# Weight conversion in two pieces through PSUM, small values in spare PSUM columns, and a new order of the work

## The chip, the cores and the metric

The kernel runs on one core of a Trainium2 chip. The time is the device time of one execution in microseconds (us); of the kernel before there are three runs, with a median of 528.46 us. Engines are called PE (TensorE), DVE (VectorE), ACT (ScalarE), POOL (GpSimd) and SP (the engine that issues the loads). Of the engines only PE, DVE and ACT work on PSUM here; POOL works on SBUF.

## The reference

Three stages follow each other on 1536 tokens (2 batches of 768) of width 320 (8 heads of 40).

```python
# stage 1: mLSTM, per batch and head, over 768 steps (written as a recurrence)
m_new = max(f + m, i);  f_s = exp(f + m - m_new);  i_s = exp(i - m_new)
C = f_s * C + i_s * outer(v, k);  n = f_s * n + i_s * k
y = sigmoid(o) * (C @ q) / max(|n . q|, 1)
# stage 2: x (1536 x 320), w_in (320 x 2048), w_out (2048 x 320)
h = x @ w_in
g = (a0 + a1*h + a2*h^2 + a3*h^3) / (1 + |b0|*|h| + |b1|*h^2 + 1e-6)
x = g @ w_out
# stage 3: w_gate, w_val (320 x 1536), w_out2 (1536 x 320)
xn = x / sqrt(mean(x*x) + 1e-6) * rms_g
out = (silu(xn @ w_gate) * (xn @ w_val)) @ w_out2
```

The weights lie in memory as 64-bit floating-point numbers (two 32-bit words for each value). The kernel makes 32-bit values of them, and of each of those a high and a low part for TensorE.

## The kernel before

**Weights.** There are 34 pieces of weight: 8 of `w_in` (key `"i"`), 8 of `w_out` (`"o"`), 12 of gate and value (`"2"`) and 6 of `w_out2` (`"3"`). Each has 640 values in each of 128 partitions and goes through `weight` (line 287): a load of 640 KB into a `raw` buffer; `c0` (line 301) and `c1` (line 307) on DVE, which shift and mask the upper word into a `cv` buffer of 640 elements; and the third step `c2`. For the 16 weights `"i"` and `"o"` it is an addition on POOL (line 325) of rounding bits that ACT prepared (`carry`, line 319); for the 18 others it is a third DVE instruction (line 312) that brings in bits of the lower word. Then ACT writes the high part (line 329) and POOL the low part (line 333). `raw` and `cv` lie in SBUF. So 34 `c0`, 34 `c1` and 18 `c2` run on DVE, each over 640 elements with every operand in SBUF.

**Attention.** 12 chunks of 128 tokens (`chunk`, line 420). A chunk has matmuls into banks named `pf`, `ps`, `pi`, `py`, `pu` and `pt`; two scans on DVE (line 435), two products (line 457); and the denominators `den_` (line 515): an absolute value on ACT, then a maximum and a reciprocal on DVE (lines 516 to 518), all in the SBUF tile `den` with 8 values in a partition. POOL uses the result in `rs` (line 522). Bank `py` goes back once `yd` has added it into the SBUF tile `yb`.

**Pairs.** Stage 2 is 48 pairs (`pair`, line 599) of 256 tokens by 256 inner columns. Each has 16 matmuls into one bank `h`, a chain on ACT, POOL and DVE, and 12 matmuls into two accumulators `acc`. Five DVE instructions of a pair (lines 645, 647, 653, 655, 657, called p2, p3, w, y2 and g) have 512 elements; p3 reads what p2 wrote, and g reads what y2 wrote. Pairs of the first two token blocks alternate, so four banks are accumulators at first, and two later on.

**Norm.** After the last pair of each of 6 blocks, `rms` (line 667): squares and a first inverse root on ACT; `newton` with five DVE instructions of two values each, in the SBUF tile `few` (lines 682 to 686); scaling on ACT (line 690), weighing on POOL, a store.

**Units.** Stage 3 is `unit` (line 754), with 512-column banks `g0` and `g1`, and sums into `acc2`.

**What sets the order.** All work is a list of 1825 tasks, and `ORDER` (line 22) is a fixed list of their numbers. Each engine runs its own tasks in that order, one after the other; SP issues loads in that order too. A task may `take` a buffer from a ring and another may `give` it back. The eight PSUM banks are one ring `"b"`; a bank is taken from the front and returned at the back, so that its next taker waits until the last one is done with it.

Of the kernel before, what the change touches and what calls it, by code (L numbers as in the profile page):

```python
# [11 lines left out]
I32 = mybir.dt.int32  # L12
# [101 lines left out]
def kernel(  # L114
# [75 lines left out]
    def T(*name):  # L190
        return held[name][1]
# [95 lines left out]
    def weight(key, src, dst, how, after=(), room=()):  # L287
# [12 lines left out]
        def c0():  # L300
            DVE.tensor_scalar(  # L301
                out=cv(), in0=words()[..., 1], scalar1=3, scalar2=0x3FFFFFFF,
                op0=ALU.logical_shift_left, op1=ALU.bitwise_and,
            )
# [702 lines left out]
```

## Time and profile before

| | us |
|---|---|
| runs: median (lowest to highest) | 528.46 (527.77 to 529.08) |
| profiled execution: its own time | 526.69 |
| its span, first to last instruction | 524.8 |
| PE busy | 464.4 |
| DVE busy | 370.1 |
| ACT busy | 305.4 |
| POOL busy | 327.9 |

Busy time is the part of the span in which an engine had at least one instruction running. Two instructions of one engine may overlap by a little in the records, so that a sum of durations can exceed the busy time. The times in the rows below count from the start of the span. A "slot" in this document is the time from the start of one DVE instruction to the start of the next.

### The profile page before, as it was taken

The page shows a single profiled execution, that of the slowest core. Times are in us where ns is not written, and L with a number is a line of the kernel's source. Part 1 is how long each engine was busy: PE and PEld are TensorE (multiplying, and loading weights), DVE is VectorE, ACT ScalarE, POOL GpSimd, SP SyncE. Part 2 cuts the span into 40 slices and gives each one's busy share as a digit, 9 for nine tenths or more (in the row PEclk, how much of TensorE's full clock was granted, in tenths as well). Part 3 has the DMA queues.
Part 4 walks back from the last instruction along what each step waited for, and adds up shares of the span by engine and source line. Part 5 has one row for each costly group of instructions (what it writes and reads, how often), then busy time and mean ns, then how long its engine had stood idle before and what let it go on. Part 6 is the DMA issues. An engine that isn't in the chain of part 4 may idle for free.

```text
span 524.8 us, 9403 instructions
## 1 busy us (share of the span) xinstructions
PE 464.4 (88%) x3616; PEld 429.3 (82%) x3616; DVE 370.1 (71%) x564; ACT 305.4 (58%) x565; POOL 327.9 (62%) x324
## 2 busy tenths in 40 slices
PE   0688976785999899998788989999999999999997
PEld 0577966675887889898687979989898988989997
DVE  7998898989999999999999999777611121111112
ACT  4243787677997787788988999583312222231112
POOL 3698887997988777678787695666750130311220
PEclk9999978898999999999999999999999999999999
DMA  8755624311012123204021115433101000000002
GB/s 255 243 145 160 205 94 136 99 59 51 26 44 65 35 56 108 70 7 139 37 82 51 51 30 179 156 96 129 56 31 50 0 14 26 1 1 9 5 1 76
DMA packets 18365, 40.40 MB, mean 77 GB/s; under 512 B 3952, under 2 KB 11904, under 8 KB 18320
## 3 DMA queue, kind: packets, MB, share of 16 engines
q1 hardware_dynamic: 18320, 39.80, 24.4%
q8 instruction: 28, 0.46, 0.4%
q14 instruction: 17, 0.14, 0.1%
HBM read 35.86 MB, written 3.93 MB: 76 GB/s over the span
## 4 chain that ended last, share of the span: by engine, by line
PE 40%; DVE 31%; ACT 17%; issue 6%; DMA 2%; POOL 2%; SPq 0%; DVEq 0%; ACTq 0%; POOLq 0%
PE bank L773 22%; PE bank L783 4%; PE bank L782 4%; PE bank L781 4%; DVE bank L655 3%; DVE z L653 3%; DVE vv L647 3%; DVE vv L645 3%; DVE cv L301 3%; DVE w_buf L435 3%; PE bank L617 3%; DVE cv L307 3%; ACT bank L650 3%; DVE vv L657 2%; ACT z L641 2%
## 5 line engine op out<-in xcount | busy, mean ns | idle before, releaser
L617 PE MATMUL bank<-xt,win 128*128 128x256 f32 x768 | 109.7, 300 | 20.1 <-DVE vv L657 10.2
L617 PEld LDWEIGHTS bank<-xt,win 128*128 128x128 f32 x768 | 102.8, 205 | 24.4 <-DVE vv L657 11.3
L849 DVE TENSOR_TENSOR vv<-bank,vv 128x512 f32<-128x512 f32 x35 | 23.7, 688 | 95.1 <-PE bank L773 80.7
L644 POOL TENSOR_TENSOR z<-z,u 128x512 f32<-128x512 f32 x48 | 64.1, 1335 | 21.7 <-ACT z L641 20.0
L661 POOL TENSOR_TENSOR gl<-vv,gh 128x512 fp32r<-128x512 f32 x48 | 64.7, 1352 | 10.9 <-ACT gh L660 6.7
L627 PE MATMUL bank<-wou,gh 128*128 128x320 f32 x192 | 60.2, 325 | 5.3 <-ACT gh L660 2.6
L629 PE MATMUL bank<-wou,gh 128*128 128x320 f32 x192 | 58.9, 318 | 0.8 <-POOL wou L333 0.8
L846 ACT ACTIVATE vv<-bank 128x512 f32<-128x512 f32 x35 | 20.8, 597 | 59.9 <-PE bank L773 51.0
L855 POOL TENSOR_TENSOR wou<-vv,wou 128x512 fp32r<-128x512 f32 x18 | 24.4, 1362 | 41.4 <-ACT wou L852 39.8
L627 PEld LDWEIGHTS bank<-wou,gh 128*128 128x128 f32 x192 | 37.6, 196 | 6.8 <-ACT gh L660 3.3
L650 ACT ACTIVATE bank<-z,few 128x512 f32<-128x512 f32 x48 | 32.8, 686 | 15.5 <-DVE vv L647 14.0
L641 ACT ACTIVATE z<-u,few 128x512 f32<-128x512 f32 x48 | 39.1, 814 | 2.1 <-DVE vv L657 1.0
L307 DVE SCALAR_TENSOR_TENSOR cv<-raw,cv 128x640 int32<-128x640 int32 x34 | 39.9, 1184 | 0.3
L629 PEld LDWEIGHTS bank<-wou,gh 128*128 128x128 f32 x192 | 37.5, 195 | 1.4 <-POOL wou L333 1.4
L627 PE MATMUL bank<-wou,gl 128*128 128x320 f32 x192 | 37.9, 320 | 0.8 <-POOL gl L661 0.6
L643 ACT ACTIVATE vv<-bank,few 128x512 f32<-128x512 f32 x48 | 32.3, 679 | 7.9 <-PE bank L617 3.2
L645 DVE SCALAR_TENSOR_TENSOR vv<-vv,few,bank 128x512 f32<-128x512 f32 x48 | 35.5, 740 | 1.5 <-ACT vv L643 0.7
L647 DVE SCALAR_TENSOR_TENSOR vv<-vv,few,bank 128x512 f32<-128x512 f32 x48 | 35.6, 743 | 0.8
L655 DVE SCALAR_TENSOR_TENSOR bank<-vv,few,bank 128x512 f32<-128x512 f32 x48 | 35.8, 747 | 0.1
L660 ACT ACTIVATE gh<-vv 128x512 fp32r<-128x512 f32 x48 | 29.7, 623 | 9.3 <-DVE vv L657 9.2
L333 POOL TENSOR_TENSOR win<-cv,win 64x128 fp32r<-64x128 f32 (+2 forms) x37 | 29.7, 803 | 7.9 <-ACT win L329 6.1
L653 DVE SCALAR_TENSOR_TENSOR z<-z,bank 128x512 f32<-128x512 f32 x48 | 32.4, 678 | 2.1 <-ACT bank L652 1.6
(156 smaller groups left out, 1163.7 us busy)
## 6 DMA issues: line engine op xcount, KB each, us to landing
raw<-in_w_out_dram SPq DMA_DIRECT2D x14, 640.0 KB, 5.0
raw<-in_w_gv_dram SPq DMA_DIRECT2D x12, 640.0 KB, 4.6
raw<-in_w_in_dram SPq DMA_DIRECT2D x8, 640.0 KB, 5.1
lqk<-in_qk_tr_dram SPq DMA_DIRECT2D x24, 192.0 KB, 4.0
lv<-in_v_dram SPq DMA_DIRECT2D x12, 160.0 KB, 4.2
los<-in_o_gate_dram SPq DMA_DIRECT2D x12, 160.0 KB, 3.3
lk<-in_k_dram SPq DMA_DIRECT2D x12, 160.0 KB, 3.2
z_dram<-rnd SPq DMA_DIRECT2D x6, 320.0 KB, 3.1
```

Of the source, the lines that this page charges most:

```text
L307: DVE.scalar_tensor_tensor(out=cv(), in0=words()[..., 1], scalar=-0x40000000, in1=cv(), op0=ALU.bitwise_and, op1=ALU.bitwise_or)
L617: PE.matmul(out=hb()[:, e], lhsT=l, rhs=r, start=(x == 0), stop=(x == len(mm) - 1))
L627: PE.matmul(out=o, lhsT=l, rhs=woh[:, f], start=first, stop=last)
L629: PE.matmul(out=o, lhsT=l, rhs=wol[:, f], start=False, stop=False)
L641: go("z", lambda: ACT.activation(out=z(), in_=u(), func=ACTF.Identity, scale=babs[:, 1:2], bias=babs[:, 0:1]), [("hu", i)], ["z"])
L644: go("zu", lambda: POOL.tensor_tensor(out=z(), in0=z(), in1=u(), op=ALU.mult), [("z", i)], [], ["u"])
L645: go("p2", lambda: DVE.scalar_tensor_tensor(out=vv(), in0=vv(), scalar=nacoef[:, 2:3], in1=hb(), op0=ALU.add, op1=ALU.mult), [("hu", i), ( ...
L647: go("p3", lambda: DVE.scalar_tensor_tensor(out=vv(), in0=vv(), scalar=nacoef[:, 1:2], in1=hb(), op0=ALU.add, op1=ALU.mult), [("p2", i)])
L650: go("ars", lambda: ACT.activation(out=hb(), in_=z(), func=ACTF.Abs_reciprocal_sqrt, bias=cq), [("zu", i), ("p3", i)])
L655: go("y2", lambda: DVE.scalar_tensor_tensor(out=hb(), in0=vv(), scalar=nacoef[:, 0:1], in1=hb(), op0=ALU.add, op1=ALU.mult), [("w", i)])
L661: go("gl", lambda: POOL.tensor_tensor(out=gl(), in0=vv(), in1=r32(gh()), op=ALU.subtract), [("gh", i)], ["gl"], ["vv"])
L773: PE.matmul(out=bank(i, e), lhsT=l, rhs=r, start=y == 0, stop=y == len(mm) - 1)
```

## The change

Four edits.

First, `c0`, `c1` and `c2` on DVE are each made twice over 320 elements. What lies between them (`mid`) is no longer in the SBUF buffer `cv` but in columns 0 to 319 of a PSUM bank that the piece takes from ring `"b"` at `c0` and gives back at its last DVE step. The last step writes `cv`. One operand, the word that was loaded, still comes from SBUF. The ACT step `carry` no longer comes after `c0`.

Second, the denominators' absolute value and maximum lie in columns 336 to 343 of bank `py`, which is now given back after the reciprocal; the three instructions become three tasks.

Third, in `newton` the mean's scaling and the first square go to ACT, and the three instructions left on DVE work on two columns of the accumulator bank.

Fourth, `ORDER` is a new list, of 1953 tasks.

```diff
+        def word(x, t):
+            return piece(T(*rk)[:, 0:1280].rearrange("p (m t) -> p m t", t=2)[..., t], x)
+        def mid(x):
+            return T("cb", key, x)[:, 0:320].bitcast(I32)
-        def c0():
+        def c0(x):
             DVE.tensor_scalar(
-                out=cv(), in0=words()[..., 1], scalar1=3, scalar2=0x3FFFFFFF,
+                out=mid(x), in0=word(x, 1), scalar1=3, scalar2=0x3FFFFFFF,
                 op0=ALU.logical_shift_left, op1=ALU.bitwise_and,
             )
-        def c1():
+        def c1(x):
             DVE.scalar_tensor_tensor(
-                out=cv(), in0=words()[..., 1], scalar=-0x40000000, in1=cv(), op0=ALU.bitwise_and, op1=ALU.bitwise_or
+                out=piece(T(*ck), x) if how > 0.5 else mid(x), in0=word(x, 1), scalar=-0x40000000, in1=mid(x),
+                op0=ALU.bitwise_and, op1=ALU.bitwise_or,
             )
-        def c2():
+        def c2(x):
             DVE.scalar_tensor_tensor(
-                out=cv(), in0=words()[..., 0], scalar=29, in1=cv(), op0=ALU.logical_shift_right, op1=ALU.bitwise_or
+                out=piece(T(*ck), x), in0=word(x, 0), scalar=29, in1=mid(x),
+                op0=ALU.logical_shift_right, op1=ALU.bitwise_or,
             )
...
+            task(("c0",) + key + (x,), lambda x=x: c0(x), [("ld",) + key] + old, take=[("b", ("cb", key, x))])
...
-            task(("cr",) + key, carry, [("c0",) + key], take=[("rnd", nk)])
+            task(("cr",) + key, carry, [("ld",) + key], take=[("rnd", nk)])
...
-        def den_():
-            ACT.activation(out=den, in_=T("yb", j)[:, :, D:D1], func=ACTF.Abs)
-            DVE.tensor_scalar(out=den, in0=den, scalar1=1.0, scalar2=None, op0=ALU.max)
-            DVE.reciprocal(out=den, in_=den)
+        def den_(x):
+            t = T("py", j)[:, 336:344, None]
+            if x == 0:
+                ACT.activation(out=t, in_=T("yb", j)[:, :, D:D1], func=ACTF.Abs)
+            elif x == 1:
+                DVE.tensor_scalar(out=t, in0=t, scalar1=1.0, scalar2=None, op0=ALU.max)
+            else:
+                DVE.reciprocal(out=den, in_=t)
...
+        def few_():
+            return T("acc", n, 0)[:, 336:338]
+            ACT.activation(out=ms, in_=ss, func=ACTF.Identity, scale=1.0 / DM, bias=eps6)
+            ACT.activation(out=few_(), in_=y, func=ACTF.Square)
         def newton():
-            DVE.tensor_scalar(out=ms, in0=ss, scalar1=1.0 / DM, scalar2=1e-6, op0=ALU.mult, op1=ALU.add)
-            DVE.tensor_tensor(out=t2, in0=y, in1=y, op=ALU.mult)
-            DVE.tensor_tensor(out=t2, in0=t2, in1=ms, op=ALU.mult)
-            DVE.tensor_scalar(out=t2, in0=t2, scalar1=-0.5, scalar2=1.5, op0=ALU.mult, op1=ALU.add)
-            DVE.tensor_tensor(out=t2, in0=t2, in1=y, op=ALU.mult)
+            t = few_()
+            DVE.tensor_tensor(out=t, in0=t, in1=ms, op=ALU.mult)
+            DVE.tensor_scalar(out=t, in0=t, scalar1=-0.5, scalar2=1.5, op0=ALU.mult, op1=ALU.add)
+            DVE.tensor_tensor(out=t2, in0=t, in1=y, op=ALU.mult)
```

## Rows read from the trace of the kernel before

**Rows 1.** The page: busy us (share of the span) of each engine, instructions

```profile
PE 464.4 (88%) x3616; PEld 429.3 (82%) x3616; DVE 370.1 (71%) x564; ACT 305.4 (58%) x565; POOL 327.9 (62%) x324
```

**Rows 2.** Busy time by stretch: length; PE, PEld, DVE, ACT, POOL; clock, DMA share, GB/s

```profile
50.00:150.00 100.00, 80.92 (x688) 75.49 (x685) 92.20 (x131) 76.31 (x135) 87.12 (x85) 0.90 0.28 90
150.00:250.00 100.00, 93.68 (x972) 86.89 (x971) 97.81 (x165) 80.39 (x151) 77.43 (x85) 1.00 0.24 72
250.00:316.00 66.00, 55.07 (x387) 51.93 (x385) 63.67 (x99) 57.88 (x113) 50.47 (x45) 0.97 0.16 48
350.00:525.00 175.00, 171.40 (x1004) 156.31 (x1002) 45.23 (x61) 44.91 (x83) 54.72 (x39) 1.00 0.10 32
```

**Rows 3.** Three DVE lines: count, min/median/max ns, first and last start

```profile
L301 DVE TENSOR_SCALAR cv<-raw x34: 473/789/1653, 8.5 to 375.8; 128x640 int32<-128x640 int32 x34
L307 DVE SCALAR_TENSOR_TENSOR cv<-raw,cv x34: 810/873/2143, 9.9 to 376.8; 128x640 int32<-128x640 int32 x34
L653 DVE SCALAR_TENSOR_TENSOR z<-z,bank x48: 635/680/690, 64.7 to 331.4; 128x512 f32<-128x512 f32 x48
```

**Rows 4.** Timeline of DVE and of POOL around 170 us: start, length

```profile
170.28 1.13 DVE L684 TENSOR_TENSOR few<-few 128x2 f32<-128x2 f32 x1
...
170.13 1.27 POOL L644 TENSOR_TENSOR z<-z,u 128x512 f32<-128x512 f32 x1
```

**Rows 5.** Instructions on tile cv by stretch: length; busy DVE, ACT, POOL

```profile
0.00:50.00 50.00, 10.21 (x12) 4.48 (x9) 17.46 (x14) 1.00 0.70 206
50.00:150.00 100.00, 23.35 (x21) 9.66 (x22) 36.42 (x33) 0.90 0.28 90
150.00:250.00 100.00, 7.16 (x6) 2.97 (x7) 6.15 (x6) 1.00 0.24 72
250.00:316.00 66.00, 16.42 (x18) 5.66 (x15) 13.54 (x18) 0.97 0.16 48
```

**Rows 6.** Groups by line and shape: busy us, mean ns | idle before

```profile
L301 DVE TENSOR_SCALAR cv<-raw 128x640 int32<-128x640 int32 x34 | 30.2, 902 | 0.2
L795 DVE COPY ob<-bank 128x320 f32<-128x320 f32 x4 | 2.0, 489 | 17.0 <-PE bank L783 17.0
L414 DVE COPY dl<-bank 128x48 f32<-128x48 f32 x1 | 0.2, 208 | 0.7 <-PE bank L413 0.7
L517 DVE TENSOR_SCALAR den<-den 128x8 f32<-128x8 f32 x12 | 5.0, 413 | 1.4 <-ACT den L516 1.4
L518 DVE RECIPROCAL den<-den 128x8 f32<-128x8 f32 x12 | 2.4, 203 | 0.4
L682 DVE TENSOR_SCALAR few<-few 128x2 f32<-128x2 f32 x6 | 3.1, 518 | 0.0
L683 DVE TENSOR_TENSOR few<-few 128x2 f32<-128x2 f32 x6 | 0.9, 154 | 0.3 <-ACT few L679 0.3
L684 DVE TENSOR_TENSOR few<-few 128x2 f32<-128x2 f32 x6 | 1.9, 323 | 0.2
L685 DVE TENSOR_SCALAR few<-few 128x2 f32<-128x2 f32 x6 | 1.0, 170 | 0.2
L686 DVE TENSOR_TENSOR few<-few 128x2 f32<-128x2 f32 x6 | 2.0, 339 | 0.2
L516 ACT ACTIVATE den<-yb 128x8 f32<-128x8 f32 x12 | 2.5, 209 | 10.9 <-POOL los L526 5.5 <-DVE yb L489 5.3
```

**Rows 7.** Timeline of DVE: w, y2 and g of one pair in a row

```profile
97.53 0.68 DVE L653 SCALAR_TENSOR_TENSOR z<-z,bank 128x512 f32<-128x512 f32 x1
98.12 0.74 DVE L655 SCALAR_TENSOR_TENSOR bank<-vv,few,bank 128x512 f32<-128x512 f32 x1
98.90 0.69 DVE L657 SCALAR_TENSOR_TENSOR vv<-z,bank 128x512 f32<-128x512 f32 x1
```

**Rows 8.** DVE's longest wait between 50 and 316 us: total, times, longest

```profile
DVE w_buf L435 <- PE bank L432: 1.9, 1, 1.9
```

More of the change, by code (lines that the diff above doesn't have):

```diff
@@ L298, in ld, with piece @@
             nc.sync.dma_start(out=words(), in_=src.bitcast(I32).rearrange("p n (f t) -> p n f t", t=2))
-        def c0():
+        def piece(t, x):
+            return t[:, x * 320:(x + 1) * 320]
+        def word(x, t):
[3 more added lines that the diff above has]
+        def c0(x):
             DVE.tensor_scalar(
-                out=cv(), in0=words()[..., 1], scalar1=3, scalar2=0x3FFFFFFF,
+                out=mid(x), in0=word(x, 1), scalar1=3, scalar2=0x3FFFFFFF,
                 op0=ALU.logical_shift_left, op1=ALU.bitwise_and,
             )
-        def c1():
+        def c1(x):
             DVE.scalar_tensor_tensor(
-                out=cv(), in0=words()[..., 1], scalar=-0x40000000, in1=cv(), op0=ALU.bitwise_and, op1=ALU.bitwise_or
+                out=piece(T(*ck), x) if how > 0.5 else mid(x), in0=word(x, 1), scalar=-0x40000000, in1=mid(x),
+                op0=ALU.bitwise_and, op1=ALU.bitwise_or,
             )
-        def c2():
+        def c2(x):
             DVE.scalar_tensor_tensor(
-                out=cv(), in0=words()[..., 0], scalar=29, in1=cv(), op0=ALU.logical_shift_right, op1=ALU.bitwise_or
+                out=piece(T(*ck), x), in0=word(x, 0), scalar=29, in1=mid(x),
+                op0=ALU.logical_shift_right, op1=ALU.bitwise_or,
             )
@@ L335, in weight @@
         task(("ld",) + key, ld, after, take=[("raw", rk)])
-        task(("c0",) + key, c0, [("ld",) + key], take=[("cv", ck)])
-        task(("c1",) + key, c1, [("c0",) + key])
+        for x in range(2):
+            old = [("c0",) + key + (0,)] if x else []
+            task(("c0",) + key + (x,), lambda x=x: c0(x), [("ld",) + key] + old, take=[("b", ("cb", key, x))])
+            old = [("c1",) + key + (0,)] if x else []
+            whole = [("cv", ck)] if not x else []
+            if how > 0.5:
+                task(("c1",) + key + (x,), lambda x=x: c1(x), [("c0",) + key + (x,)] + old, take=whole,
+                     give=[("cb", key, x)])
+            else:
+                task(("c1",) + key + (x,), lambda x=x: c1(x), [("c0",) + key + (x,)] + old)
+                old = [("c2",) + key + (0,)] if x else []
+                task(("c2",) + key + (x,), lambda x=x: c2(x), [("c1",) + key + (x,)] + old, take=whole,
+                     give=[("cb", key, x)] + ([rk] if x else []))
         if how > 0.5:
-            task(("cr",) + key, carry, [("c0",) + key], take=[("rnd", nk)])
-            task(("c2",) + key, add, [("c1",) + key, ("cr",) + key], give=[rk, nk])
+            task(("cr",) + key, carry, [("ld",) + key], take=[("rnd", nk)])
+            task(("c2",) + key, add, [("c1",) + key + (1,), ("cr",) + key], give=[rk, nk])
         else:
-            task(("c2",) + key, c2, [("c1",) + key], give=[rk])
+            task(("c2",) + key, None, [("c2",) + key + (1,)])
         three = key[0] in ("i", "2")
@@ L513, in ca @@
                     DVE.tensor_copy(out=cc, in_=t[r])
-        def den_():
-            ACT.activation(out=den, in_=T("yb", j)[:, :, D:D1], func=ACTF.Abs)
-            DVE.tensor_scalar(out=den, in0=den, scalar1=1.0, scalar2=None, op0=ALU.max)
-            DVE.reciprocal(out=den, in_=den)
+        def den_(x):
[4 more added lines that the diff above has]
+                DVE.tensor_scalar(out=t, in0=t, scalar1=1.0, scalar2=None, op0=ALU.max)
+            else:
+                DVE.reciprocal(out=den, in_=t)
         def rs():
@@ L564, in chunk @@
             ("yd", j), yd, [("y", j)] + ([("ys", j)] if ch else []),
-            take=[] if ch else [("yb", ("yb", j))], give=[("py", j)],
+            take=[] if ch else [("yb", ("yb", j))],
         )
@@ L573, in chunk @@
             task(("ca", j), ca, [("u", j)] + ([("cd", j)] if ch else [("yi", j - 1)] if j else []), give=[("pu", j)])
-        task(("den", j), den_, [("yd", j)] + prev("rs"))
+        task(("den0", j), lambda: den_(0), [("yd", j)])
+        task(("den1", j), lambda: den_(1), [("den0", j)])
+        task(("den", j), lambda: den_(2), [("den1", j)] + prev("rs"), give=[("py", j)])
         task(("rs", j), rs, [("den", j), ("sig", j)])
```

181 rows, old and new, of the table ORDER are left out of this document.

## The prediction

> **What bounds the kernel now.** I read the busy times first [rows 1]: PE 464.4 us and DVE 370.1 of a span of 524.8. An average hides stages, so the busy times by stretch came next [rows 2]. There the reader is to see two regimes. From 50 to 316 us DVE has work for 92.2 of 100, 97.8 of 100 and 63.7 of 66 us, and PE is idle for 19.1, 6.3 and 10.9 us. From 350 us on PE is busy for 171.4 of 175 us and DVE for 45.2: nothing that DVE saves there can shorten the run. 316 us is about where the first stage-3 matmuls start. So the change is worth what it takes off DVE before 316 us, and at most what PE has idle there: 36.3 us between 50 and 316.
>
> Third I looked at how long single DVE instructions take [rows 3]. L653, with one operand in SBUF and one in PSUM, takes 635 to 690 ns in all its 48 cases. L301 and L307, with SBUF alone, run from 473 to 1653 and from 810 to 2143 ns. Why, the timeline shows [rows 4]: L684, two elements wide, starts behind POOL's L644, takes 1.13 us and ends at 171.41; L644 ends at 171.40. An all-SBUF DVE instruction ends here when POOL's does; L653 beside it never has such a tail. The Trainium skill (SBUF — State Buffer, "Who interferes with whom") has the same: a port pair shared by VectorE and GpSimd is locked for a whole instruction, by a VectorE instruction with two SBUF inputs or in a two-port mode; these rows agree, 1.13 us against a mean of 170 ns for the like L685 [rows 6].
>
> **The conversions.** On the tile cv, DVE spends 10.2, 23.4, 7.2 and 16.4 us in the four stretches up to 316 us, 57.1 us for 57 instructions [rows 5]. Followed through its task numbers, the new order has 45 c0, 45 c1 and 13 c2 pieces ahead of the first stage-3 matmul, 103 in all; in the old one 24, 24 and 8 whole instructions stand there, so 1.5 weights are put off as well. No row shows a DVE instruction that reads one SBUF operand and writes PSUM. The nearest with 320 elements is L795, a copy out of PSUM: 489 ns [rows 6]. How much of that counts depends on what follows [rows 7]: L655 starts 0.59 us after L653 of 0.68 us, an overlap of 0.09; L657, which reads what L655 wrote, starts 0.78 us after it, 0.04 more than its 0.74. So a piece has a slot of 0.40 us if its successor is independent and 0.53 if not. In the new order 24 of 172 pieces have the next step of the same piece right behind them: 0.40 + 0.13 x 24/172 = 0.42 us. 103 x 0.42 = 43.3, a saving of 13.8 us. The bounds: every slot at 0.53 gives 54.6, a saving of 2.5; a c0 piece at half of L301's minimum, 0.24, and the others at 0.40 give 45 x 0.24 + 58 x 0.40 = 34.0, a saving of 23.1. I take 0.42, from the row of the same size. Most of the gain is c1: two pieces with slots of 0.42 against a median of 873 ns are no gain, it lies in the long tail. Each c0 that POOL doesn't disturb gets slower, from 473 ns to two of 0.42 us. The Trainium skill (VectorE: DVE Perf Modes, "Why PSUM operands drop a tier") has this as a rule: an fp32 instruction with a PSUM operand loses the doubled rate. By it the sum stays where it is; if it did not hold for a PSUM output, the saving would be the 23.1.
>
> **Small values.** The two denominators' instructions take 0.413 and 0.203 us, 12 times; the nearest small one with PSUM is L414, 208 ns [rows 6]. 12 x (0.616 - 0.416) = 2.4 us. The norm's five, L682 to L686, take 0.518 + 0.154 + 0.323 + 0.170 + 0.339 = 1.50 us; three at 0.208 are left, and 5 of 6 norms come before 316 us: 5 x 0.88 = 4.4 us. ACT gets two more there, 2 x 0.209 by L516, or 2.1 us in five norms. I charge nothing for them: in that chain the two DVE steps that they replace took 0.67 us on average against 0.42. If ACT is late without that cover, 2.1 us is the price.
>
> **The order.** It does one thing that rows can price. In the old order p3 stands directly behind its p2 23 times and g behind its y2 27 times; in the new one 2 and 5 times. 43 fewer dependent neighbours at 0.13 us are 5.6 us. The price of an order at large can't be read off. At the start I bound it by the loads: 4.26 MB instead of 3.30 lie ahead of the third chunk's q and k on SP's queue, 4.7 us later at the 206 GB/s of the first 50 us [rows 5]; for the fourth it is 5.42 instead of 6.54, 5.4 us sooner. I take zero.
>
> **What is added.** Each c0 piece takes a PSUM bank and so may wait, and behind it on DVE stands everything: p2 to g of the pairs, on which PE waits. I followed the bank ring through the new list. Of 68 pieces, 62 get a bank that a DVE task gave back last, which costs DVE no wait, 3 a bank not used before, and 3 one from ACT. Bank `py` is held through two small instructions more. For both together, and for pairs' matmuls that find fewer free banks, I set 3 us. Half-length instructions also hold up p2 to g for less time, which I don't count.
>
> **The sum.** DVE saves 13.8 + 2.4 + 4.4 + 5.6 = 26.2 us before 316 us. By stretch: 0.7 up to 50 us, 8.2 in 50 to 150, 7.7 in 150 to 250 and 9.4 in 250 to 316 (conversions by [rows 5] with pieces at 0.42 us; norms three and two in the last two stretches; the rest by the pairs in each). Against PE's idle time [rows 2]: the 8.2 fits into 19.1, whole; of 7.7 I count 3, half of the 6.3 that PE has free; of 9.4 I count 5, half of 10.9, since ACT is busy for 57.9 of 66 us too. That is 16, less 3 for banks: 13 us. The profiled execution took 526.7 us; 513.7 would be left. The median of the runs lies 1.8 us above it, so 515.5 us.
>
> **Rivals.**
> *All of it arrives.* A busy PE is not PE at its peak, and PE gets its clock, 0.90 in 50 to 150 us, back: 528.5 - 26 = 502.5 us. For it: L301 and L307 are long exactly where pairs wait for p2. Against: PE's 6.3 us in 150 to 250.
> *PE and ACT take over.* PE is at 94% in 150 to 250 us. If only the stretch from 50 to 150 gives, and half of that, 4 us remain: 524.5. Against: DVE is the fullest engine in all three stretches.
> *Bank waits, the other sign.* The new order lets pieces take banks while four accumulators and several `h` are out. One in-order DVE queue then waits for PE or ACT, which it hardly does now: the longest is 1.9 us [rows 8]. It decides from 13/45 = 0.29 us per c0 piece ahead of 316 us; at 0.45 us it costs 20, and the time is 528.5 - 13 + 20 = 535.5 us. Against: the 62 of 68.
> *The change doesn't do what it says.* A c0 piece still reads SBUF alone; if it still waits for POOL, each costs what L301 costs above its minimum, its mean of 902 ns less 473, 0.43 us [rows 3, 6], 45 x 0.43 = 19: 534.5 us. Against: L653, with a PSUM operand, never does.
>
> **How the numbers follow.** Forecast 0.50; all arrives 0.13; PE and ACT 0.20; bank waits 0.10; c0 still blocked 0.07. What a measurement can tell from no change is 0.3%, 1.6 us. Faster gets the forecast, all arrives, and 0.14 of the PE case: 0.77. Within: 0.06 of the PE case and 0.02 of the last two: 0.08. Slower: 0.15. The likeliest case alone spans 508 (c0 pieces at 0.24, order 5 us better) to 521 (every slot 0.53). The range for 8 in 10 goes from 506, short of the case where all arrives, to 530, with most of the PE case and a start 5 us worse.
>
> **What would show it.** Right: pieces of 0.45 to 0.50 us with hardly any spread, no L301 or L307 above 0.6 us; DVE's busy time at least 15 us down; PE's idle time between 50 and 316 us at 20 to 25; the first stage-3 matmul near 303 us. Wrong: DVE's waits for `bank` at c0 in the list of waits; c0 pieces near 0.9 us; or PE idle as before with ACT or POOL named as its releaser.

## The result: 497.2 us, faster by 31

The changed kernel takes 497.17 us (median of four runs, 496.07 to 498.04) against 528.12 for the kernel before beside it: a ratio of 0.942, with a 95% interval of 0.938 to 0.946. The forecast was 515.5, with a range from 506 to 530. The direction came as predicted; the gain is more than twice what was predicted, and the time lies below the range.

The page of the changed kernel gives each engine's busy time, its share of the span of 495.5 us (the execution itself took 497.63), and its instructions:

```profile
PE 459.8 (93%) x3616; PEld 424.9 (86%) x3616; DVE 338.0 (68%) x638; ACT 308.9 (62%) x579; POOL 313.5 (63%) x324
```

Against [rows 1] DVE has 32.1 us less, POOL 14.4 less, PE 4.6 less and ACT 3.5 more. The stretches of [rows 2], in the changed kernel:

```profile
50.00:150.00 100.00, 88.61 (x794) 82.14 (x793) 94.19 (x169) 91.07 (x168) 93.04 (x96) 0.95 0.27 84
150.00:250.00 100.00, 97.04 (x960) 91.30 (x959) 96.96 (x175) 88.67 (x167) 77.59 (x83) 1.00 0.22 63
250.00:316.00 66.00, 62.79 (x478) 60.95 (x478) 60.37 (x119) 60.06 (x117) 54.29 (x55) 1.00 0.41 129
```

PE is now idle for 11.4, 3.0 and 3.2 us there, 17.6 in place of 36.3. But fixed stretches hold other work in the two kernels, since the changed one is ahead. A better cut is by milestones that both have: the ends of the first, the 45th and the last of the 48 g (L657 before, L691 after). The columns are those of [rows 2]; first the kernel before:

```profile
0.00:70.60 70.60, 46.68 (x518) 41.44 (x518) 61.92 (x102) 32.81 (x64) 51.97 (x69) 0.99 0.65 195
70.60:310.70 240.10, 208.99 (x1817) 195.43 (x1817) 230.40 (x358) 197.01 (x363) 193.74 (x190) 0.95 0.21 66
310.70:333.50 22.80, 21.01 (x166) 20.73 (x166) 21.84 (x32) 17.56 (x32) 16.24 (x17) 1.00 0.46 160
333.50:524.80 191.30, 187.73 (x1118) 171.71 (x1117) 55.92 (x77) 57.98 (x107) 65.97 (x51) 1.00 0.12 38
```

and the changed kernel, from milestone to milestone:

```profile
0.00:64.30 64.30, 46.45 (x493) 40.70 (x493) 55.34 (x117) 32.15 (x60) 47.78 (x68) 1.00 0.68 208
64.30:284.40 220.10, 205.71 (x1855) 193.24 (x1853) 211.58 (x383) 201.34 (x377) 187.54 (x189) 0.98 0.24 73
284.40:302.50 18.10, 18.10 (x141) 18.09 (x142) 17.69 (x36) 17.58 (x32) 13.23 (x15) 1.00 0.52 156
302.50:495.50 193.00, 189.54 (x1132) 172.91 (x1131) 53.34 (x106) 57.87 (x111) 64.94 (x55) 1.00 0.13 42
```

The second column is the length, the fifth is DVE. The three stretches up to the last g became 6.3, 20.0 and 4.7 us shorter, and DVE's busy time in them fell by 6.6, 18.8 and 4.2. In total what DVE saved up to the last g, 29.6 us, came through (31.0); the rest of the span grew by 1.7. About 2.5 of the 29.6 are work put off and not saved: 120 of the 172 pieces are done by the last g, where the kernel before had done 63 of its 86 whole instructions, as much as 126 pieces, and a piece adds 0.41 us. Behind the last g DVE is busy for only 53 of 193 us. In what follows "the middle stretch" is the one from the first to the 45th g: 240.1 us with 230.4 of DVE before, 220.1 with 211.6 after.

Where DVE's time went. These are the conversion lines of the changed kernel (count, min/median/max ns, first and last start), the answer to [rows 3]:

```profile
L317 DVE TENSOR_SCALAR bank<-raw x68: 473/486/497, 8.5 to 340.5; 128x320 int32<-128x320 int32 x68
L323 DVE SCALAR_TENSOR_TENSOR cv<-raw,bank x32: 435/482/489, 9.6 to 126.0; 128x320 int32<-128x320 int32 x32
L323 DVE SCALAR_TENSOR_TENSOR bank<-raw,bank x36: 484/492/498, 200.3 to 341.0; 128x320 int32<-128x320 int32 x36
L329 DVE SCALAR_TENSOR_TENSOR cv<-raw,bank x36: 476/481/489, 202.0 to 341.6; 128x320 int32<-128x320 int32 x36
```

The tails up to 2143 ns are gone: no piece is longer than 498 ns. The small values, by line and shape (busy us, mean ns | idle before), answer to L517 and L682 to L686 of [rows 6]:

```profile
L548 DVE TENSOR_SCALAR bank<-bank 128x8 f32<-128x8 f32 x12 | 2.0, 168 | 0.3 <-ACT bank L546 0.3
L723 DVE TENSOR_TENSOR bank<-bank,few 128x2 f32<-128x2 f32 x6 | 1.0, 164 | 2.9 <-ACT bank L719 2.9
L724 DVE TENSOR_SCALAR bank<-bank 128x2 f32<-128x2 f32 x6 | 1.0, 168 | 0.2
L725 DVE TENSOR_TENSOR few<-bank,few 128x2 f32<-128x2 f32 x6 | 1.0, 159 | 0.2
```

A maximum of 413 ns on average became 168; the two-element instructions that are left on DVE, up to 339 ns on average before, take 159 to 168. The Trainium skill (SBUF — State Buffer, "Who interferes with whom") says that a VectorE instruction with at most one SBUF input, outside the two-port modes, doesn't contend with GpSimd. These rows agree, with a spread of 24 ns over 68 pieces. The Trainium skill (VectorE: DVE Perf Modes, "Why PSUM operands drop a tier") says that any PSUM operand rules out the two-port modes and leaves an fp32 instruction at the plain rate. This case agrees for 32-bit integers written to PSUM: 473 ns at the least here against 286 for the same piece within SBUF (below).

POOL gains too. Its multiplication in a pair (L644 before, L678 after) lost its tail as well, though the change doesn't touch it:

```profile
L644 POOL TENSOR_TENSOR z<-z,u x48: 1267/1296/1910, 60.9 to 328.4; 128x512 f32<-128x512 f32 x48
```

```profile
L678 POOL TENSOR_TENSOR z<-z,u x48: 1270/1297/1332, 54.2 to 294.4; 128x512 f32<-128x512 f32 x48
```

With the pieces in SBUF again (below) its longest is 1571 ns. So the meetings of DVE and POOL had cost both, and part of the 14.4 us that POOL has less is this. How much of the gain came by way of POOL, no run separates; POOL is busy for 194 of 240 us in the middle stretch before.

DVE's longest waits between the first and the last g of the changed kernel (total us, times, longest), the answer to [rows 8]:

```profile
DVE z L687 <- ACT bank L686: 2.3, 6, 0.6
DVE vv L679 <- ACT u L674: 1.3, 5, 0.6
DVE bank L723 <- ACT bank L719: 1.2, 2, 0.7
```

No wait of a c0 for a bank is among these or behind them in the list.

### The profile page after: what moved, and what is told of

Same layout as the page of the kernel before. It is cut to its first block, busy times and chain, and to the rows that moved or that the text cites. A ratio compares the mean times of both kernels' runs of the same rounds, so it can differ in the third digit from the quotient of the medians.

```text
span 495.5 us, 9528 instructions
## 1 busy us (share of the span) xinstructions
PE 459.8 (93%) x3616; PEld 424.9 (86%) x3616; DVE 338.0 (68%) x638; ACT 308.9 (62%) x579; POOL 313.5 (63%) x324
## 4 chain that ended last, share of the span: by engine, by line
PE 60%; DVE 16%; ACT 13%; issue 4%; POOL 4%; DMA 2%; DVEq 0%; ACTq 0%; POOLq 0%
PE bank L812 24%; PE bank L651 9%; PE bank L661 6%; PE bank L822 4%; PE bank L820 4%; PE bank L821 4%; PE bank L663 3%; DVE w_buf L463 2%; DVE vv L681 2%; ACT u L674 2%; DVE vv L679 2%; ACT gh L694 2%; ACT vv L677 2%; ACT bank L684 2%; PE bank L513 2%
## 5 line engine op out<-in xcount | busy, mean ns | idle before, releaser
L651 PE MATMUL bank<-xt,win 128*128 128x256 f32 x768 | 106.4, 293 | 9.3 <-DVE xt L630 3.3
L651 PEld LDWEIGHTS bank<-xt,win 128*128 128x128 f32 x768 | 99.1, 198 | 12.9 <-DVE xt L630 3.7
L695 POOL TENSOR_TENSOR gl<-vv,gh 128x512 fp32r<-128x512 f32 x48 | 62.0, 1296 | 15.5 <-ACT gh L694 9.3
L678 POOL TENSOR_TENSOR z<-z,u 128x512 f32<-128x512 f32 x48 | 62.2, 1296 | 14.7 <-ACT z L675 12.6
L661 PE MATMUL bank<-wou,gh 128*128 128x320 f32 x192 | 59.0, 319 | 2.7 <-DVE cst L539 1.1
L663 PE MATMUL bank<-wou,gh 128*128 128x320 f32 x192 | 57.2, 310 | 0.0
L894 POOL TENSOR_TENSOR gl<-vv,wou 128x512 fp32r<-128x512 f32 x10 | 12.9, 1295 | 51.2 <-ACT wou L891 51.1
L894 POOL TENSOR_TENSOR wou<-vv,wou 128x512 fp32r<-128x512 f32 x13 | 16.8, 1295 | 40.2 <-ACT wou L891 40.2
L661 PEld LDWEIGHTS bank<-wou,gh 128*128 128x128 f32 x192 | 36.4, 189 | 4.7 <-ACT gh L694 1.8
L663 PEld LDWEIGHTS bank<-wou,gh 128*128 128x128 f32 x192 | 36.4, 190 | 0.0
L317 DVE TENSOR_SCALAR bank<-raw 128x320 int32<-128x320 int32 x68 | 32.8, 487 | 1.7 <-DMA raw<-in_w_gv_dram 1.6
L691 DVE SCALAR_TENSOR_TENSOR vv<-z,bank 128x512 f32<-128x512 f32 x48 | 32.8, 683 | 0.3
```

Source lines behind the costliest of these rows:

```text
L651: PE.matmul(out=hb()[:, e], lhsT=l, rhs=r, start=(x == 0), stop=(x == len(mm) - 1))
L661: PE.matmul(out=o, lhsT=l, rhs=woh[:, f], start=first, stop=last)
L663: PE.matmul(out=o, lhsT=l, rhs=wol[:, f], start=False, stop=False)
L678: go("zu", lambda: POOL.tensor_tensor(out=z(), in0=z(), in1=u(), op=ALU.mult), [("z", i)], [], ["u"])
L695: go("gl", lambda: POOL.tensor_tensor(out=gl(), in0=vv(), in1=r32(gh()), op=ALU.subtract), [("gh", i)], ["gl"], ["vv"])
```

## The experiments

The question: why did more than twice the predicted gain arrive? The first theory, A in the expectations, is that the place in memory alone shortens DVE's instructions and that DVE sets the pace, so that what DVE saves arrives whole. Its rivals, B, are that the new order, the halved length or another engine's pace has a large part in it. Each expectation gives the numbers of both; the last four runs ask the narrower question whether ACT or PE sets the pace, and there A says that it does in the changed kernel, and that it doesn't in the kernel before. The table has each run's time, its ratio to the kernel before in the same session, and its middle stretch. The changed kernel itself wasn't run again in those sessions: where a run is set against it below, the difference is one of medians from two sessions, and by the ratios it would be up to 1 us higher.

| | us | ratio, 95% interval | middle: length | DVE busy |
|---|---|---|---|---|
| before | 528.1 | 1 | 240.1 | 230.4 |
| after | 497.2 | 0.942 [0.938, 0.946] | 220.1 | 211.6 |
| old memory, new order | 536.9 | 1.017 [1.014, 1.020] | 246.4 | 230.5 |
| new memory, old order | 545.2 | 1.033 [1.030, 1.036] | 251.3 | 220.6 |
| pieces in SBUF | 536.7 | 1.018 [1.016, 1.020] | 238.1 | 227.5 |
| small values in SBUF | 503.2 | 0.954 [0.952, 0.956] | 226.0 | 218.9 |
| dependent neighbours | 504.5 | 0.958 [0.956, 0.960] | 227.5 | 218.6 |
| c1 twice | 514.9 | 0.977 [0.974, 0.980] | 229.7 | 224.0 |
| fewer c1 | 496.9 | 0.943 [0.941, 0.946] | 220.3 | 206.9 |
| fewer neighbours | 500.2 | 0.949 [0.947, 0.951] | 221.5 | 211.0 |
| sigmoids together | 497.0 | 0.942 [0.940, 0.945] | 219.1 | 211.3 |
| the last, and fewer c1 | 496.5 | 0.941 [0.938, 0.944] | 218.5 | 206.7 |
| fewer matmuls, changed kernel | 492.1 | 0.933 [0.930, 0.937] | 216.2 | 210.5 |
| fewer matmuls, kernel before | 527.9 | 1.000 [0.998, 1.002] | 239.8 | 230.2 |

### Each half of the change alone

**Old memory, new order.** The instructions of before, whole and in SBUF, in the new order; `carry` comes after the load as in the changed kernel.

```diff
-            task(("cr",) + key, carry, [("c0",) + key], take=[("rnd", nk)])
+            task(("cr",) + key, carry, [("ld",) + key], take=[("rnd", nk)])
-ORDER = (before's)
+ORDER = (the new one; a whole instruction stands at its first piece)
```

> The conversions are whole again (640 elements, SBUF alone), the small values too; the tasks follow the new order (a few conversion steps come later, where no cv buffer is free). Theory A (DVE's own time, and nearly all of it reaches the end): only the order's share stays, 5.6 us for the dependent neighbours and about 6 us at the start, so 514 to 519 us. Rival B (the new order is what counts, the memory little): 505 us or less.

Measured: 536.9, 1.7% slower than before. Both expectations missed. DVE's busy time in the middle stretch is what it was, but the stretch is 6.3 us longer: DVE is idle in it for 16.0 us in place of 9.7. And single instructions changed. Two that became longer, in this kernel (count, min/median/max):

```profile
L302 DVE SCALAR_TENSOR_TENSOR cv<-raw,cv x18: 811/1409/2090, 232.0 to 384.7; 128x640 int32<-128x640 int32 x18
L507 DVE TENSOR_SCALAR den<-den x12: 156/571/1231, 28.1 to 263.0; 128x8 f32<-128x8 f32 x12
```

The mean of the third conversion step rose from 1111 to 1389 ns, that of the denominators' maximum from 413 [rows 6] to 616; that of c0 fell from 902 to 848, and that of c1 from 1184 to 1172. So what the same instruction in the same memory loses to POOL depends on the order, in either direction. The means in [rows 6], by which the prediction priced what the change would remove, hold for the old order alone.

**New memory, old order.** The changed instructions in the order of before; 106 of the 1953 tasks had to go later for lack of a free bank.

```diff
-ORDER = (the new one)
+ORDER = (before's; all pieces of a weight close together where its last step stood, later where no bank is free)
```

> Pieces through PSUM and small values in PSUM as in the changed kernel, tasks in the old order (both pieces directly behind each other at the place of the old last step; 106 of 1953 steps have something put off because no bank is free). Theory A: the memory's share stays, 13.8 us for conversions and 6.8 us for small values, so 505 to 511 us. Rival B: 518 us or more.

Measured: 545.2, 3.3% slower than before, although DVE has 9.8 us less to do in the middle stretch and each piece is as short as in the changed kernel. The waits of PE in this kernel, from 50 to 330 us (total, times, longest):

```profile
PE bank L639 <- DVE cv L317: 11.9, 3, 7.9
PE bank L639 <- DVE cv L311: 9.0, 4, 3.9
```

L317 and L311 are the last DVE steps of pieces, which give banks back, and L639 is the first matmuls of pairs: they wait 20.9 us in 7 waits for banks that pieces hold. The third rival of the prediction had DVE wait for banks; here it is mostly PE that waits, for banks that pieces still hold, in an order that isn't made for pieces; c0 itself waits for a bank for 4.4 us in 2 waits (64 to 335 us). So neither half gains: 1.7% and 3.3% are lost alone, 5.8% gained together. Neither run is a pure half, though: in the first c0 needs a `cv` buffer again, which the new order doesn't plan for, and in the second the pieces of a weight stand closer together than its steps did. How much a planner of the order could have had from old memory can't be told from these runs.

### The parts of the new memory

**Pieces in SBUF.** The changed kernel with what lies between c0, c1 and c2 in the `cv` buffer again; the bank is still taken and given back. `cv` has to be taken at c0, one or two steps earlier, so 12 of the 1953 tasks stand elsewhere, and c0 can wait for that ring.

```diff
         def mid(x):
-            return T("cb", key, x)[:, 0:320].bitcast(I32)
+            return piece(T(*ck), x)
...
```

> The changed kernel, but what lies between a piece's steps is in SBUF (the piece of cv that it ends in) and not in PSUM; the bank is taken all the same, small values stay in PSUM, order as new as the cv ring allows. Theory A: pieces of 0.24 (c0) and 0.48 us with POOL's tails on top again, some 0.35 us on most of them, twice as many instructions as before: 515 to 530 us. Rival B: 500 us or less, since c0 even gets its double rate back.

Measured: 536.7, 39.6 above the changed kernel, more than either theory allowed. The three steps in this kernel:

```profile
L305 DVE TENSOR_SCALAR cv<-raw x68: 286/328/1675, 8.7 to 383.3; 128x320 int32<-128x320 int32 x68
L311 DVE SCALAR_TENSOR_TENSOR cv<-raw,cv x68: 458/516/1894, 9.6 to 383.6; 128x320 int32<-128x320 int32 x68
L317 DVE SCALAR_TENSOR_TENSOR cv<-raw,cv x36: 477/492/1749, 218.0 to 384.1; 128x320 int32<-128x320 int32 x36
```

The medians are like those in PSUM, for c0 even shorter; the maxima are three times that and more. Groups of these lines come to 40.4, 54.7 and 29.1 us, 124.2 in all, against 82.8 in the changed kernel. The halved length is kept here and the gain is gone, so it is the place, not the length, that keeps these instructions short. Not all of the 39.6 us is the place, though: c0 also waits 9.7 us for POOL to give `cv` buffers back, the longest group of these waits is

```profile
DVE cv L305 <- POOL w2gv L338: 4.4, 2, 2.3
```

Up to the last g the run is 29.4 us longer, with 27.3 more of DVE.

**Small values in SBUF.** The changed kernel with the denominators and the norm's three steps in SBUF.

```diff
-            t = T("py", j)[:, 336:344, None]
+            t = den
...
-            return T("acc", n, 0)[:, 336:338]
+            return t2
```

> The changed kernel with the denominators (12 times) and the norm's three DVE instructions (6 times) in SBUF again; two norm steps stay on ACT. Theory A: up to 12 x 0.2 + 5 x 0.5 = 5 us of tails come back, 499 to 502 us. Rival B: 497 us, no change that can be measured.

Measured: 503.2, 6.0 above the changed kernel, with 9.1 us more of DVE on the page (347.1 against 338.0). The maximum in this kernel:

```profile
L548 DVE TENSOR_SCALAR den<-den x12: 163/663/1265, 26.0 to 241.2; 128x8 f32<-128x8 f32 x12
```

It takes 663 ns at the median for 8 values in a partition, against 168 in a bank. Theory A, a little above its range.

### What a microsecond of DVE is worth

**Dependent neighbours.** The changed kernel with p3 directly behind its p2 and g behind its y2, without other work between: 124 such neighbours in place of 31.

```diff
-ORDER: ... p2(j), a piece or a step of another pair, p3(j) ...
+ORDER: ... p2(j), p3(j), that piece or step ...
```

> The changed kernel with p3 moved directly behind its p2 and g directly behind its y2 in all 48 pairs. The number of DVE instructions that stand directly behind the one whose result they read (p2 to p3, y2 to g, c0 to c1, c1 to c2) goes from 31 to 124. Theory A (DVE's slots set the time, 0.12 us for each such neighbour): 93 x 0.12 = 11 us, so 506 to 510 us. Rival B (other engines are near their limit too, a slot of DVE no longer counts): 497 to 500 us.

Measured: 504.5, 7.3 above, or 0.08 us for each of 93. DVE's busy time in the middle stretch rose by 7.0 and its length by 7.4. The term of the prediction (0.13 us for one) was right in kind.

**c1 twice.** Each c1 piece is issued twice, with the same result.

```diff
-            DVE.scalar_tensor_tensor(
+            for _ in range(2):
+                DVE.scalar_tensor_tensor(
...
```

> The changed kernel with each c1 piece issued twice (same result): 68 more DVE instructions, 51 of them before the last pair's g, at slots of 0.40 to 0.53 us. Theory A (DVE sets the time up to the last pair, one to one): 51 x 0.42 to 0.53 = 21 to 27 us more, 518 to 524 us. Rival B (half of it is hidden, as the prediction took it): 507 to 511 us.

Measured: 514.9, 17.7 above, between the two ranges. The middle stretch of this kernel:

```profile
69.20:298.90 229.70, 207.72 (x1853) 194.42 (x1853) 223.96 (x412) 202.00 (x377) 188.74 (x189) 0.97 0.23 70
```

12.4 more of DVE made it 9.6 longer, 0.77 for one. DVE's idle time paid the rest: 5.7 in place of 8.5.

**Fewer c1.** The other direction: c1 is left out for the 18 weights of stage 3, whose values are then wrong.

```diff
-                task(("c1",) + key + (x,), lambda x=x: c1(x), [("c0",) + key + (x,)] + old)
+                task(("c1",) + key + (x,), None, [("c0",) + key + (x,)] + old)
```

> The changed kernel without c1 for the 18 weights of stage 3 (the sign and top exponent bits are left out, so these weights are wrong): 36 DVE pieces fewer, 19 of them before the last pair's g. Theory A (DVE still sets the time after the change): 19 x 0.41 = 8 us less, 488 to 491 us. Rival B (PE, at 94% of 300 us, has taken over): 494 to 497 us.

Measured: 496.9, no gain; the rival B. The middle stretch of this kernel and its longest wait of DVE, from 64 to 304 us:

```profile
64.60:284.90 220.30, 206.86 (x1852) 195.57 (x1849) 206.93 (x371) 201.33 (x378) 186.83 (x188) 0.96 0.24 73
```

```profile
DVE z L687 <- ACT bank L686: 4.5, 9, 0.8
```

DVE has 4.7 us less to do, and the stretch is as long as before. The time that DVE saves it now waits. So "DVE sets the pace" holds from the kernel before to about here, and no further.

**Fewer neighbours.** 17 tasks of the new order moved by one place each, which leaves 8 dependent neighbours of 31.

```diff
-ORDER: ... y2(j), g(j), other ...
+ORDER: ... y2(j), other, g(j) ...
```

> The changed kernel with 17 tasks moved by one place on DVE, so that 8 instead of 31 instructions stand directly behind the one whose result they read. Theory A: 23 x 0.12 = 2.8 us less, 494 to 495 us, if the instruction put between is ready in time. Rival B: no change, or a little slower since it isn't ready: 497 to 499 us.

Measured: 500.2, 3.0 above: the direction of rival B, just above its range. DVE's busy time in the middle fell by 0.5 only, while DVE's idle time there rose from 8.5 to 10.5. What moved is now late for its reader; which of the 17 moves cost it wasn't tried.

**Sigmoids together**, and the same with fewer c1. Four sigmoids of the attention (and three loads ahead of them) stand earlier, beside other sigmoids, so that ACT loads its tables four times less. Two such loads in the changed kernel, on ACT's timeline (start, length):

```profile
98.11 1.28 ACT L564 ACT_TABLE_LOAD   x1
...
101.30 1.28 ACT L684 ACT_TABLE_LOAD   x1
```

```diff
-ORDER: ... pair steps, sigmoid(c), pair steps, sigmoid(c+1) ...
+ORDER: ... sigmoid(c), sigmoid(c+1), pair steps ...
```

> The changed kernel with the four sigmoids (chunks 9, 5, 11 and 10) that stand among the pairs moved ahead of the first pair's inverse root, and three loads of o_gate earlier: four of ACT's table loads, 4 x 1.28 us, go. Theory A (after the change ACT, PE and DVE are all near their limit, ACT the one that hid what the run without c1 saved): 2 to 5 us less, 492 to 495 us. Rival B (PE alone is the limit now, or the earlier loads hold up q and k at the start): 497 us or more.

> The same, and without c1 for the 18 weights of stage 3 (sign and top exponent bits left out, so these weights are wrong), as in the run without c1. Theory A (ACT was in the way of DVE's saving): a further 3 to 8 us less than the run with the sigmoids together, 486 to 491 us. Rival B (PE is the limit): the same time as that run.

Measured: 497.0 and 496.5, no gain that can be told from none; the rival B in both. ACT's page time fell from 308.9 to 303.9, and with the c1 left out DVE's fell to 323.2; the middle stretch is 219.1 and 218.5 long against 220.1.

### Whether PE is the limit

The prediction had cut 26 us to 16 because PE was busy for 94% from 150 to 250 us. PE's longest wait of the kernel before, from 50 to 330 us, speaks for DVE: the first matmuls of pairs (L617) wait for the bank that a g gives back.

```profile
PE bank L617 <- DVE vv L657: 10.2, 4, 5.1
```

The direct test takes PE's work away: 4 of the 16 first matmuls of a pair, 192 in all. What they would add is left out of the result.

```diff
                     (whi[:, a, c0:c0 + 128], xt[:, 0, a]),
-                    (whi[:, a, c0:c0 + 128], xt[:, 1, a]),
                     (wli[:, a, c0:c0 + 128], xt[:, 0, a]),
```

**From the kernel before:**

> The kernel before without the same 192 matmuls. Theory A (DVE was the limit before, PE was not): 524 us or more, at most 3 us less. Rival B (PE was near its limit already, as the prediction took it for half of DVE's saving): 505 to 518 us.

Measured: 527.9, a ratio of 1.000. The middle stretch of that kernel:

```profile
68.70:308.50 239.80, 196.50 (x1642) 180.50 (x1642) 230.17 (x357) 196.97 (x364) 194.25 (x190) 0.92 0.21 66
```

PE lost 12.5 us of busy time there and the stretch is 0.3 shorter. PE at 87% of this stretch, and 94% in its fullest part, held nothing back, as theory A has it. That DVE's 230 of 240 us did is argued from this and from the runs with more DVE work; no run takes work from DVE alone in the kernel before.

**From the changed kernel:**

> The changed kernel without 4 of the 16 matmuls into h of each pair (the products of the high weight with the low part of x are left out, so the result is less exact): 192 matmuls of 256 columns, some 0.12 us each, 23 us of PE's work in the stretch of the pairs. Theory A (after the change PE is the limit, since neither DVE's nor ACT's saving moved the time): 5 to 20 us less, 477 to 492 us. Rival B (no engine is the limit but the length of a pair's chain and the order): 495 us or more.

Measured: 492.1, 5.0 less than the changed kernel. The stretch from 150 to 250 us in this run, beside the one shown above:

```profile
150.00:250.00 100.00, 91.94 (x893) 84.19 (x894) 99.40 (x181) 91.72 (x172) 80.52 (x85) 1.00 0.22 66
```

PE has 17.4 us less on the page (442.4 against 459.8), 5.0 of it arrives, and DVE is then at 99.4 of 100. Now PE does limit a little; the time is just above theory A's range of 477 to 492. Taken with the runs above: the changed kernel stands about where its engines set the pace together. A microsecond more of DVE in the middle stretch makes it 0.8 to 1.1 longer (5.9 for 7.3, 7.4 for 7.0, 9.6 for 12.4); less of DVE, or of ACT, or of both brought nothing that can be measured; less of PE is worth a part.

No version that computes the whole reference came out below the changed kernel by more than can be told from no change.

## Why the prediction was wrong

**What bounds the kernel: right.** As far as the runs show, DVE set the pace of the kernel before, up to the last g, and nothing in the last 190 us gained.

**The sum of what DVE saves: near in total, by luck.** 26.2 us were forecast before the first stage-3 matmul; from the start to the 45th g DVE's busy time fell by 25.4 (61.92 + 230.40 - 55.34 - 211.58). But it lies elsewhere: 0.7 was forecast up to 50 us and 25.3 from there to 316, and 6.6 came before the first g and 18.8 in the middle stretch. By parts, counted as what an instruction adds to DVE's busy time when its overlap with the one before is taken off (together 25.7; all else took 0.3 more):
- The conversions gave 9.6, not 13.8. The slot of a piece is right: 103 pieces up to the 45th g added 42.0 us, 0.41 each, against 0.42. But the prediction set 103 pieces against 56 whole instructions, which are 112 pieces; 9 of them, 3.8 us, were put off and not saved. And 57.1 us was a sum with overlaps. Up to the 45th g the kernel before had done 53 whole ones, which added 51.6.
- The norm gave 5.3, not 4.4, and the denominators 3.9, not 2.4: with an operand in a bank the norm's three and the maximum take 0.16 to 0.17 us, not the 0.208 of L414.
- The neighbours, p3 and g, gave 2.7, not 5.6: by the run with 93 more of them one costs 0.08 us, not 0.13, and 43 x 0.08 = 3.4.
- The gates at the start gave 4.2, which had no term; 3.2 of it are their scans. These are all-SBUF as before; the group in the kernel before, and then in the changed one:

```profile
L397 DVE TENSOR_TENSOR_SCAN scr<-scr,zc 16x128 f32<-16x128 f32 x6 | 5.3, 932 | 0.1
```

```profile
L425 DVE TENSOR_TENSOR_SCAN scr<-scr,zc 16x128 f32<-16x128 f32 x6 | 2.1, 397 | 0.1
```

POOL's first large instruction starts at 10.89 us before and at 15.08 after; the scans start between 10.8 and 19.0 before and between 10.1 and 13.2 after. They are over before POOL begins. PE's wait for these scans, 12.5 us before, is 0.3 after. Short scans alone don't bring the start forward: with old memory in the new order they come to 2.1 us too, and the first g ends at 72.7 us, against 70.6 before and 64.3 after.

**The step that failed: from DVE's saving to the time.** It read: "of 7.7 I count 3, half of the 6.3 that PE has free; of 9.4 I count 5, half of 10.9, since ACT is busy for 57.9 of 66 us too. That is 16, less 3 for banks: 13 us." The two halves rested on no row. Removing 192 matmuls from the kernel before changed nothing, so PE's 94% was no limit. The half on account of ACT wasn't tested in the kernel before; the measured saving speaks against it. And PE had the room: it is idle for 31.1 us of the middle stretch before and 14.4 after. In that stretch DVE's busy time fell by 18.8 us and the length by 20.0. The halves hid that the sum for this stretch was too large: without them 25.3 less 3 for banks would have stood against the 20.0. The 3 us for banks can't be found as a loss either: no c0 waits for a bank among DVE's longest waits, and PE waits 4.8 us in 6 waits from 50 to 303 us for banks that pieces hold, within its idle time; the longest group is

```profile
PE bank L651 <- DVE cv L329: 2.3, 2, 1.8
```

**Two terms that were left at zero.** At the start "I take zero" by the loads; the first g ends 6.3 us sooner. After 316 us nothing was counted; the last three pairs, with conversions and norm between them, became 4.7 us shorter and the rest 1.7 longer. So the miss of 16.3 us (29.3 of span against 13) is 7.0 in the middle, 6.3 at the start and 3.0 at the end.

**The rivals.** "All of it arrives", at 502.5 us with a chance of 0.13, was the nearest. Its first reason fits, a PE at 94% was no limit; its second, PE's clock, isn't shown to matter: in 50 to 150 us the granted clock rose from 0.90 to 0.95, but with fewer matmuls in the kernel before it was 0.86 there and the time the same. Its time lacks the start and the end. "PE and ACT take over" came true only behind the gain: the runs with less of DVE or ACT show it in the changed kernel. "Bank waits" didn't come with the new order; a relative of it, PE waiting for banks that pieces hold, is seen with the old order at 545 us. A c0 that POOL still blocks is excluded by 68 pieces of 473 to 497 ns.

**The signs that were named.** Pieces of 0.45 to 0.50 us and DVE at least 15 us down: 0.435 to 0.498, and 32.1 on the page. PE's idle time from 50 to 316 us at 20 to 25: 17.6. First stage-3 matmul near 303 us: 282.0. None of the three signs of being wrong appeared.

## What to carry to other kernels

Two engines that are both over 90% busy in a stretch needn't share the limit, as here: before cutting a gain because "the other is full too", take work off the other one and see whether the time moves. Where POOL works all along, as here, intermediate values of DVE in a PSUM bank kept its instructions at the same duration every time, though c0 undisturbed is faster within SBUF; but banks held by such pieces are missing elsewhere, so order and memory had to be changed together. What a contention costs in one order is not what it costs in another.

## What the runs showed of the hardware

- An instruction of 2 or 8 values in a partition can take 1.2 us: the maximum over 128x8 in SBUF took from 163 to 1265 ns, and from 154 to 175 with its operand in a bank.
- The same 320 values shifted and masked by c0 took 286 ns at the least within SBUF, 473 from SBUF into PSUM; yet the kernel with the slower of the two places was 39.6 us faster, a part of that through the other's waits for `cv` buffers.
- POOL's instructions pay for the meetings too: the same multiplication over 128x512 took up to 1910 ns in the kernel before and at most 1332 in the changed one.
- PE with less work got a lower clock: with fewer matmuls in the kernel before the granted clock of the middle stretch was 0.92 against 0.95, and over the whole span 0.951 to 0.961 in all ten runs against 0.967 to 0.977 for the kernel before beside it. The time was the same.
